# A gated mix of linear attention and a Fourier block on one core: stores, adds and accumulators moved within a hand-written order

## The chip, the core and the metric

The kernel runs on one core of a Trainium2 chip. The metric is the device time of one execution in microseconds (us), as the median of several runs. TensorE (PE in the profile) multiplies matrices out of SBUF into PSUM; VectorE (DVE) and ScalarE (ACT) work element by element; GpSimd (POOL) and SyncE (SP) issue DMA transfers here. Every engine works through its own list of instructions in the order of that list, so an instruction that waits holds up all that stand behind it on the same engine.

## What is computed

The reference, cut to what matters (S = 2048 rows, D = 576 columns, 32 heads of 18):

```python
g = sigmoid((x * gate_w).sum(-1))
q, k, v = split(x @ wqkv)                       # per head
pq, pk = phi(q), phi(k)                         # phi(t) = t+1 if t>0 else exp(t); + 1e-6
o = (pq @ (pk.T @ v)) / (pq @ sum(pk) + 1e-6)   # linear attention
a = o @ wo
b = Cr @ (x @ Wr.T) - Ci @ (x @ Wi.T)           # real part of a 2-d Fourier transform
out = g * a + (1 - g) * b
```

## The kernel before, in words

Every float32 product is made out of three products of split operands: each operand is written as a high part (made by ScalarE, `hi_of`, L179) and a low part (VectorE subtracts, `lo_of`, L189), and high x high, high x low and low x high are added up in PSUM. Four of the products (q, and those with W_r, W_i, Cr and Ci) are also done by a scheme with seven products in place of eight half-size ones: left and right operands are combined by adds on VectorE first (`add`, L199), into seven "forms". A group of rows t and its partner t + 8 make a pair; there are eight pairs.

The stages in order of time:

1. k's product for 16 row groups, and the gate (L574, L209).
2. The product with x of the k-features, 20 steps (five column groups c of x times four groups q of rows; L754). Each step loads a chunk (`xg_load`), makes its high part on ScalarE (`xg_next`) and queues its low part, which VectorE does at the next step's `tick()`. TensorE reads a chunk two steps after its high part was queued. Beside this run, step by step, the preparations for later stages: `turn` says at which step which of four generators goes on by one piece: `a`, `b`, `c` are the three parts of W_q (`right_here`: load, adds, adds, high part, low part in two pieces), `x` is the form of pair 6, `p` the form of the remainders (32 columns of each half, stored to DRAM).
3. q's product in 56 slots (`q_slot`, TensorE at L929), seven products for each of eight pairs, taken in four "quads" of two pairs: (6, 2), (3, 4), (0, 5), (7, 1). Each slot is seven matmuls, under a microsecond. What comes out of PSUM goes through sums on VectorE, an exponential on ScalarE (L938, or L942 and L943) and a last operation on VectorE (L939, L944) into one of 16 accumulators `acc` of [128, 576]. `plan` says behind which slot what else is queued: the forms of pairs 7, 0 and 1 (`left[k]`, five pieces each: two adds, two adds, high part, two low parts; their loads are `begin_left`, L366 on POOL), the stores of forms to DRAM (`here[k].store`, L398 on POOL, seven DMAs for a pair, held until the last exponential queued so far is done), the normalising steps (`norm`), and `m`, the splitting of the output matrix M (five parts; two of them end in an accumulating DMA on POOL, L909, the last one is the remainder's high part on ScalarE and low part on VectorE).
4. The output product, 16 iterations i (L1345 on): the next accumulator is transposed on TensorE (L840), split into qs (ScalarE, VectorE), multiplied with M (L209), scaled into `acc[i]` by ScalarE (L1356) and stored to `att` (L1358, on POOL). `hidden.make_w(k)` makes the seven parts of W_r at given iterations (high part on ScalarE, low part on VectorE), and SyncE loads remainders (`load_rest`, L1111) and forms (`load_pair`, `load_x`, L1117) for the next stage.
5. The product of x with W_r (L1134), that with Cr (L1290), and the same with W_i and Ci.

SBUF is one arena, and every tile's place is an offset given by hand. Dependences follow from overlapping places: whoever writes a place waits for all that still read it. The accumulators lie in a row from ACC_AT, 2,304 bytes each; pair 6's form lies at ACC_AT + 22784, so it overlaps accumulators 9 to 15. The third quad's results are accumulators 8 to 11, the fourth's 12 to 15. W_r's parts have seven places, of which `Layout.w` picks one for each part; place 4 covers SLOT_AT + 43776 to 49536, place 6 SLOT_AT + 32256 to 38016. The remainder of pair 2 is loaded to T_AT + 60416.

The order on ScalarE, VectorE and SyncE is as written in the program; on TensorE it is as written in the q product and from the W_r product on. Elsewhere, and on POOL, a planner sets it.

Of the kernel before, what the change touches and what calls it, by code (L numbers as in the profile page):

```python
# [8 lines left out]
F = mybir.dt.float32  # L9
# [5 lines left out]
P = 128  # L15
S, D, H, DH = 2048, 576, 32, 18
# [51 lines left out]
T_AT = 0  # L68
ACC_AT = T_AT + NP * TPAIR
SLOT_AT, SLOT = ACC_AT + NT * D * 4 + 256, 7 * BS * P * 4  # L70
# [21 lines left out]
class Layout:  # L92
# [32 lines left out]

    def w(self, k):
        if not self.swap:
            k = (k + 4) % 7
        if k < 4:
            return WF_AT + k * WF  # L130
        if self.swap and k == 6:
            return SLOT_AT + 3 * SLOT
        return SLOT_AT + 14 * XF + XR + (6 - k) * WF + (1024 if self.swap else 0)
# [3 lines left out]
def kernel(  # L137
# [24 lines left out]
    def at(offset, shape, dtype=F, name="t"):  # L162
        count[0] += 1
        t = nc.alloc_sbuf_tensor_at(f"{name}_{count[0]}", list(shape), dtype,
                                    offset=base + offset)
        return t.ap()
# [8 lines left out]
    def bank():  # L175
        return psum.tile([P, 512], F, tag="bank", name="bank")
# [17 lines left out]
    def tick():  # L194
        while pending:
            pending.pop(0)()
# [9 lines left out]
    def run(ps, pairs):  # L206
        pairs = list(pairs)
        for n, (a, b) in enumerate(pairs):
            nc.tensor.matmul(ps, a, b, start=(n == 0), stop=(n == len(pairs) - 1))  # L209

    def half(h):
        return slice(h * HALF, (h + 1) * HALF)
# [37 lines left out]
    acc = [at(ACC_AT + i * D * 4, [P, D], F, "acc") for i in range(NT)]  # L250
# [26 lines left out]
    def steps(xs, rhs):  # L277

        for c in range(KC):
            yield xs[:, c], rhs(c)  # L280
            yield xs[:, c], rhs(5 + c)
            yield xs[:, 5 + c], rhs(c)
        yield xs[:, 4], rhs(4)
        yield xs[:, 9], rhs(4)
# [169 lines left out]
    def right_here(src, rest, places, last, temp):  # L454
# [3 lines left out]
        def piece(k):  # L458
# [24 lines left out]
            else:  # L483
                rows = slice(32, 64)
                lo_of(hi[rows], r[rows], hi[rows])

        return w, [piece(k) for k in range(3)]

    def right_raw(src, rest, o, o_rest):
# [21 lines left out]
    def go(gen, n=1):  # L511
        for _ in range(n):
            next(gen, None)
# [7 lines left out]
    done = []  # L521
# [174 lines left out]
    here, forms, rests = {}, {}, {}  # L696

    def begin_left(k, o):
        here[k] = Left(k, o, done[-1])
        if k < NP:  # L700
            forms[k] = here[k].c
# [8 lines left out]
    def load_rest_q(p, o, queue=nc.sync):  # L710
        rests[p] = at(o, [P, 7, P], R, "xr")
        n = min(NP * 96 - p * 96, P)
        queue.dma_start(out=rests[p].bitcast(F)[:n], in_=xrest[p * 96:p * 96 + n])
# [6 lines left out]
    def load_two(*places):  # L720
        for p, o in places:
            forms[p] = at(o, [P, 7, 2, 2 * P], R, "xf")
        for a, b in ((2, 4), (0, 2), (4, 7)):
# [2 lines left out]

    turns = dict(p=rest_forms(), a=wq_pieces[0], b=wq_pieces[1], c=wq_pieces[2], x=left_of(6, False))
    turn = {4: "p", 5: "p", 6: "p", 7: "p", 8: "pap", 9: "pa", 10: "paxc", 11: "pxpaac",
            12: "pcxcb", 13: "xbb", 14: "b", 15: "x", 17: "b"}

    plan = {
        2: [lambda: begin_left(NP, ACC_AT)],
# [100 lines left out]
    def transposed(i):  # L833

        xs, _ = new_xs("qs", qs_ring)
        banks = [bank(), bank()]
        twice = twices.pop(0)
        for c in range(5):
            a = acc[i][:, c * P:(c + 1) * P] if c < KC else twice.rearrange("p a b -> p (a b)")
            nc.tensor.transpose(banks[c // KC][:, (c % KC) * P:(c % KC + 1) * P], a, ident)  # L840
        hi_of(xs[:, 0:4], banks[0])
        lo_of(xs[:, 5:9], banks[0], xs[:, 0:4])
        hi_of(xs[:, 4], banks[1][:, :P])
        lo_of(xs[:, 9], banks[1][:, :P], xs[:, 4])
        return xs
# [68 lines left out]
    def m_row(h, j):  # L914
        return ms["hi"][:, j, half(h)] if j <= KC else ms["lo"][:, j - 5, half(h)]
# [16 lines left out]
    def q_feature(t, h, src, plus):  # L932
        dst = acc[place[t]][:, half(h)]

        def act():
            e = at(es.next(), [P, HALF], F, "e")
            if plus:
                done.append(nc.scalar.activation(e, src, AF.Exp, bias=less))  # L938
                dves.append(lambda: nc.vector.scalar_tensor_tensor(  # L939
                    dst, e, 1.0, src, op0=ALU.min, op1=ALU.max))  # L940
                return
            nc.scalar.activation(e, src, AF.Relu, scale=-1.0)  # L942
            done.append(nc.scalar.activation(e, e, AF.Exp, scale=-1.0))  # L943
            dves.append(lambda: nc.vector.scalar_tensor_tensor(  # L944
                dst, src, 0.0, e, op0=ALU.max, op1=ALU.add))

        feats.append(act)

    def q_slot(n, s, q):
# [35 lines left out]
        elif q == 3:  # L985
            add(sa, x, sa)
            q_feature(p, 1, sa, 1)

    pz_ring.at = [SLOT_AT + 47488]
    for g in (0, 1, 4):  # L990
        load_wo(g)
# [6 lines left out]
    def spread():  # L998
# [17 lines left out]
        16: [lambda: move_m(2), lambda: move_m(0, nc.gpsimd), lambda: move_m(3)],  # L1016
        17: [lambda: move_m(4), lambda: move_m(1, nc.gpsimd)],
        25: [lambda: begin_left(1, T_AT + 35840)],
        26: [lambda: here[6].store(slice(0, 4), done[-1]),
             lambda: here[6].store(slice(4, 7), done[-1])],  # L1020
        30: [spread],
        31: [lambda: load_rest_q(7, T_AT + 80384), lambda: load_rest_q(1, T_AT + 108928)],
        44: [lambda: here[7].store(slice(0, 4), done[-1]),
             lambda: here[7].store(slice(4, 7), done[-1])],
    }
    for k, what in ((7, (10, 11, 13, 15, 20)), (0, (13, 15, 18, 20, 23)),
                    (1, (31, 35, 36, 36, 38)), (None, (25, 27, 30, 41, 43, 45, 48, 48, 49, 52)),
                    ("m", (24, 30, 28, 34, 33))):
        for n, j in enumerate(what):
            f = norm if k is None else m_parts[n] if k == "m" else lambda k=k: go(left[k])  # L1030
            plan.setdefault(j, []).append(f)
# [51 lines left out]
    class Hidden:  # L1083
# [45 lines left out]
        def product(self, ps, p, k, start):  # L1129
            x, (w, wl) = self.x[p, k], self.w[k]  # L1130
            ops = [(x[:, a, c * P:c * P + P], w[:, 2 * c + b]) for c in range(2) for a, b in FULL]
            ops.append((self.rest[p][:96, 6 - k], wl[:96]))
            for n, (a, b) in enumerate(ops):
                nc.tensor.matmul(ps, a, b, start=(start and n == 0), stop=(n == len(ops) - 1),  # L1134
                                 skip_group_check=True)
# [209 lines left out]
    for i, t in enumerate(seq):  # L1345
        qs = nxt
        if i:
            go(norms)
        if i + 1 < NT:
            nxt = transposed(i + 1)  # L1350
        if not i:
            go(norms)
        for h in range(2):
            ps = bank()
            run(ps[:, :HALF], steps(qs, lambda j: m_row(h, j)))
            done.append(nc.scalar.activation(acc[i][:, half(h)], ps[:, :HALF], AF.Copy,  # L1356
                                             scale=gate[:, t:t + 1]))
        nc.gpsimd.dma_start(out=att[t], in_=acc[i])  # L1358
        go(norms)
        tick()  # L1360
        if i == 0 or 2 < i < 7:
            go(wr_make)
        for k, j in ((1, 2), (1, 3), (0, 4), (0, 5)):
            if i == j:
                here[k].store((slice(0, 4), slice(4, 7))[j % 2], done[-1])
        for k, j in enumerate((7, 8, 9, 10, 11, 12, 14)):
            if i == j:
                hidden.make_w(k)
        if i == 4:
            hidden.load_pair(1)  # L1370
        for p, j in ((0, 7), (1, 8), (2, 11), (3, 15)):
            if i == j:
                hidden.load_rest(p)
        if i == 11:
            hidden.load_pair(2)
        if i in (13, 15):
            for k in (0, 2) if i == 13 else (4, 6):
                hidden.load_x(3, k)
# [57 lines left out]
def _layouts(inputs):  # L1436
# [27 lines left out]
    def right(w):  # L1464

        main, rest = halves(w)
        quarters = ((0, 0), (1, 0), (1, 1), (0, 1))
        cols = (slice(0, HALF), slice(HALF, D))
        main = np.stack([main[d][:, :, cols[c]] for d, c in quarters], axis=2)
        rest = np.stack([rest[d][:, cols[c]] for d, c in quarters], axis=1)  # L1470
        return main, np.concatenate([rest] * 3)
# [44 lines left out]
```

## Time and profile before

| what | us |
|---|---|
| median of 3 runs | 721.76 |
| the runs | 721.05 to 722.81 |
| the profiled execution | 724.75 |
| its span, first to last instruction | 723.0 |
| stage 2 (x with the k-features) on TensorE | 65.6 to 132 |
| q's product | 132 to 191 |
| output product | 191 to 258.7 |
| W_r's product | 258.7 to 311.3 |

The profile is of one execution, so durations and times of day ("at 176.5") are of that execution, counted from its first instruction. A row of the timeline reads: start, duration of the group, engine and line, operation, what is written and read, shapes, count, and in brackets how long the engine stood idle before it and what ended that wait. A "landing" is the time from the start of a DMA's issue to its last byte.

### The profile page before, as it was taken

What the parts mean: (1) busy time and instruction counts of PE and PEld (TensorE: products, weight loads), DVE (VectorE), ACT (ScalarE), POOL (GpSimd) and SP (SyncE); (2) the same over time, 40 slices, a digit from 0 to 9 for tenths busy, and PEclk for the clock granted to TensorE, in tenths of its full rate; (3) what the DMA queues carried; (4) which work ended last, traced back from release to release, by engine and by line L of the source; (5) the groups of instructions that cost most, each with busy time, mean ns of one, the idle gap of its engine ahead of it and who ended that gap; (6) DMA issues with size and microseconds to landing.
All of it is one profiled execution on the core that took longest, in us unless ns stands there. A gap on an engine that the chain in (4) does not pass through costs nothing.

```text
span 723.0 us, 13795 instructions
## 1 busy us (share of the span) xinstructions
PE 715.7 (99%) x5390; PEld 714.7 (99%) x5390; DVE 594.8 (82%) x993; ACT 331.1 (46%) x507; POOL 79.0 (11%) x141
## 2 busy tenths in 40 slices
PE   9999999999999999999999999999999999999997
PEld 9999999999999999999999999999999999999997
DVE  5799996477999748899889899757889988788884
ACT  6898355577545535454334233323535333232230
POOL 1122431123252100000010000000000000000000
PEclk9999999999999999999999999999999999999999
DMA  7375799979389557454476666899954543454540
GB/s 257 108 261 190 257 348 323 335 261 250 119 271 411 224 198 276 131 183 144 130 241 209 238 209 208 290 325 400 372 188 136 167 152 123 136 167 154 153 153 34
DMA packets 54093, 157.85 MB, mean 218 GB/s; under 512 B 6884, under 2 KB 9348, under 8 KB 54028
## 3 DMA queue, kind: packets, MB, share of 16 engines
q1 hardware_dynamic: 42524, 117.23, 47.9%
q0 software_dynamic: 11216, 39.32, 15.6%
q8 instruction: 43, 0.70, 0.4%
q10 hardware_dynamic: 288, 0.41, 0.2%
q14 instruction: 22, 0.18, 0.1%
HBM read 117.80 MB, written 36.49 MB: 213 GB/s over the span
## 4 chain that ended last, share of the span: by engine, by line
PE 92%; DMA 3%; DVE 2%; ACT 1%; issue 0%; POOL 0%; DVEq 0%; POOLq 0%
PE bank L1290 49%; PE bank L209 15%; PE bank L1134 15%; PE bank L754 6%; PE bank L929 4%; PE bank L574 2%; PE bank L840 1%; DMA wraw<-in_wq_dram 1%; DMA xm<-xb 1%; DMA xb<-in_xq_dram 1%; ACT xb L179 1%; DVE xb L189 1%; PE bank L235 1%; DVE xb L199 0%; DVE sum L199 0%
## 5 line engine op out<-in xcount | busy, mean ns | idle before, releaser
L1290 PE MATMUL bank<-fh,c 128*128 128x288 f32 x1792 | 355.8, 295 | 0.0
L1290 PEld LDWEIGHTS bank<-fh,c 128*128 128x128 f32 x1792 | 285.9, 188 | 0.1
L1290 PE MATMUL bank<-fl,c 128*128 128x288 f32 x896 | 262.8, 293 | 0.0
L179 ACT ACTIVATE c<-craw 128x1792 fp32r<-128x1792 f32 (+1 forms) x84 | 121.1, 1447 | 171.5 <-DVE craw L199 164.0
L1290 PEld LDWEIGHTS bank<-fl,c 128*128 128x128 f32 x896 | 168.7, 188 | 0.0
L189 DVE TENSOR_TENSOR c<-craw,c 128x1792 fp32r<-128x1792 f32 (+4 forms) x86 | 142.0, 1653 | 1.5 <-ACT c L179 1.4
L199 DVE TENSOR_TENSOR craw<-craw 128x256 f32<-128x256 f32 (+1 forms) x192 | 98.2, 512 | 22.0 <-DMA craw<-in_ci_dram 10.6
L1134 PE MATMUL bank<-wf,xf 128*128 128x288 f32 x630 | 98.5, 296 | 0.0
L1134 PEld LDWEIGHTS bank<-wf,xf 128*128 128x128 f32 x630 | 90.0, 189 | 0.0
L209 PE MATMUL bank<-mw,qs 128*128 128x288 f32 x448 | 63.2, 298 | 0.0
L754 PE MATMUL bank<-pk,c 128*128 128x288 f32 x448 | 61.6, 296 | 1.3 <-DVE c L189 1.3
L754 PEld LDWEIGHTS bank<-pk,c 128*128 128x128 f32 x448 | 60.1, 188 | 1.5 <-DVE c L189 1.5
L209 PEld LDWEIGHTS bank<-mw,qs 128*128 128x128 f32 x448 | 59.9, 188 | 0.1
L209 PE MATMUL bank<-wd,xs 128*128 128x288 f32 (+1 forms) x336 | 44.7, 295 | 0.0
L209 PEld LDWEIGHTS bank<-wd,xs 128*128 128x128 f32 x336 | 44.6, 188 | 0.0
L199 DVE TENSOR_TENSOR ys<-bank,ys 128x288 f32<-128x288 f32 x63 | 28.8, 457 | 17.3 <-PE bank L1290 14.3
L189 DVE TENSOR_TENSOR fl<-fl,fh 128x864 fp32r<-128x864 f32 (+1 forms) x32 | 34.7, 1093 | 6.7 <-ACT fh L179 5.4
L179 ACT ACTIVATE fh<-fl 128x864 fp32r<-128x864 f32 (+1 forms) x32 | 29.8, 949 | 16.4 <-DVE fl L199 16.4
L398 POOL DMA_DIRECT2D xm<-xb x56 | 30.4, 549 | 27.7 <-ACT sum L970 7.9
L1134 PE MATMUL bank<-wf,xr 96*128 96x288 f32 x112 | 33.3, 298 | 0.0
L199 DVE TENSOR_TENSOR ys<-ys,bank 128x288 f32<-128x288 f32 x47 | 21.2, 450 | 13.0 <-PE bank L1290 12.4
L1312 ACT ACTIVATE ys<-bank 128x288 f32<-128x288 f32 x16 | 6.6, 415 | 54.9 <-PE bank L1290 54.9
(133 smaller groups left out, 807.9 us busy)
## 6 DMA issues: line engine op xcount, KB each, us to landing
xf<-xm SPq DMA_DIRECT2D x49, 512.0 KB, 9.0
craw<-in_cr_dram SPq DMA_DIRECT2D x32, 512.0 KB, 3.6
craw<-in_ci_dram SPq DMA_DIRECT2D x32, 512.0 KB, 3.7
xm<-xb POOLq DMA_DIRECT2D x56, 256.0 KB, 4.9
xr<-xr SPq DMA_DIRECT2D x21, 448.0 KB, 8.4
craw<-in_xg_dram SPq DMA_DIRECT2D x20, 256.0 KB, 5.8
att<-acc POOLq DMA_DIRECT2D x16, 288.0 KB, 3.1
row<-att SPq DMA_DIRECT2D x16, 288.0 KB, 4.2
```

Of the source, the lines that this page charges most:

```text
L179: return nc.scalar.activation(dst, src, AF.Copy, bias=bias)
L189: nc.vector.tensor_tensor(out=dst, in0=src, in1=hi, op=ALU.subtract)
L199: nc.vector.tensor_tensor(out=dst, in0=a, in1=b, op=op)
L209: nc.tensor.matmul(ps, a, b, start=(n == 0), stop=(n == len(pairs) - 1))
L235: nc.tensor.matmul(warm[:, :P], ones_f, ones_f, start=True, stop=True)
L398: ins = nc.gpsimd.dma_start(out=xforms[self.k][:, f], in_=self.c.bitcast(F)[:, f])
L574: nc.tensor.matmul(ps[i], x[:, i * P:(i + 1) * P], wkt.row(h, j), start=(c == 0 and n == 0), stop=(c == KC and n == 1))
L754: nc.tensor.matmul(ps[h][:, :HALF], t[:, a, k], pk[s][:, b, half(h)], start=(s == 0 and n == 0), stop=(s == NT - 1 and n == len(passes) - 1))
L840: nc.tensor.transpose(banks[c // KC][:, (c % KC) * P:(c % KC + 1) * P], a, ident)
L929: nc.tensor.matmul(ps, a, b, start=(start and n == 0), stop=(stop and n == len(ops) - 1), skip_group_check=True)
L1134: nc.tensor.matmul(ps, a, b, start=(start and n == 0), stop=(n == len(ops) - 1), skip_group_check=True)
L1290: nc.tensor.matmul(ps[q], c[x][:, l, k], factors[p](y, f), start=(p == 0 and i == 0), stop=(p == NP - 1 and i == 2))
```

## The change

It has five parts:

- `turn`: W_q's part `b` goes on at steps 13 (twice), 14, 15 and 17; before, at 12, 13 (twice), 14 and 17. Its first adds come behind the step-13 low part of x's chunk and behind a piece of pair 6's form.
- Accumulators 9, 10 and 11 get places of their own: SLOT_AT + 47488, T_AT + 62720 and T_AT + 60416.
- The stores of pair 6's form are queued behind slot 36; before, behind slot 26.
- Pair 1's form: second adds behind slot 33 (before 35), high part behind 35 (before 36). The last part of M's split goes behind slot 40 (before 33).
- W_r's parts 0 and 2 exchange places, part 3 is made at iteration 9 and part 2 at iteration 10 (before, the other way round). Part 2's new place overlaps that of accumulator 9.

```diff
     def w(self, k):
         if not self.swap:
-            k = (k + 4) % 7
+            k = (6, 5, 4, 0, 1, 2, 3)[k]
...
     turn = {4: "p", 5: "p", 6: "p", 7: "p", 8: "pap", 9: "pa", 10: "paxc", 11: "pxpaac",
-            12: "pcxcb", 13: "xbb", 14: "b", 15: "x", 17: "b"}
+            12: "pcxc", 13: "xbb", 14: "b", 15: "xb", 17: "b"}
...
+    for i, o in ((9, SLOT_AT + 47488), (10, T_AT + 62720), (11, T_AT + 60416)):
+        acc[i] = at(o, [P, D], F, "acc")
     pz_ring.at = [SLOT_AT + 47488]
...
         25: [lambda: begin_left(1, T_AT + 35840)],
-        26: [lambda: here[6].store(slice(0, 4), done[-1]),
-             lambda: here[6].store(slice(4, 7), done[-1])],
         30: [spread],
         31: [lambda: load_rest_q(7, T_AT + 80384), lambda: load_rest_q(1, T_AT + 108928)],
+        36: [lambda: here[6].store(slice(0, 4), done[-1]),
+             lambda: here[6].store(slice(4, 7), done[-1])],
...
-                    (1, (31, 35, 36, 36, 38)), (None, (25, 27, 30, 41, 43, 45, 48, 48, 49, 52)),
-                    ("m", (24, 30, 28, 34, 33))):
+                    (1, (31, 33, 35, 36, 38)), (None, (25, 27, 30, 41, 43, 45, 48, 48, 49, 52)),
+                    ("m", (24, 30, 28, 34, 40))):
...
-        for k, j in enumerate((7, 8, 9, 10, 11, 12, 14)):
+        for k, j in enumerate((7, 8, 10, 9, 11, 12, 14)):
             if i == j:
                 hidden.make_w(k)
```

## The prediction

> **What bounds the kernel now.** I read the page first, then the waits of TensorE, then the rows in order of time around each wait.
>
> ```profile
> PE 715.7 (99%) x5390; PEld 714.7 (99%) x5390; DVE 594.8 (82%) x993; ACT 331.1 (46%) x507; POOL 79.0 (11%) x141
> ...
> PE bank L754 <- DVE c L189: 1.3, 1, 1.3
> ...
> PE bank L929 <- DVE xb L189: 1.2, 1, 1.2
> ```
>
> TensorE works 99% of the span, and no matmul goes or shortens in this change. Behind the start only these two waits stand to be won, so the case is two places of about 1.5 us each, and what is late next at each.
>
> **First place, W_q's adds (steps 12 to 15).** TensorE, then VectorE:
>
> ```profile
> 113.73 0.76 PE L754 MATMUL bank<-pk,c 128*128 128x288 f32 x4
> 115.81 8.29 PE L754 MATMUL bank<-pk,c 128*128 128x288 f32 x60 [1.31 <-DVE c L189]
> ...
> 109.86 2.25 DVE L189 TENSOR_TENSOR wb<-wraw,wb 32x2016 fp32r<-32x2016 f32 x1 [1.41 <-ACT wb L179]
> 114.19 0.95 DVE L199 TENSOR_TENSOR wraw<-wraw 128x288 f32<-128x288 f32 x2 [2.09 <-DMA wraw<-in_wq_dram]
> 115.06 0.69 DVE L189 TENSOR_TENSOR c<-craw,c 128x512 fp32r<-128x512 f32 x1
> 115.67 1.22 DVE L189 TENSOR_TENSOR xb<-xb,xb 128x1024 fp32r<-128x1024 f32 x1
> ```
>
> Step 14 starts at 113.73, issues four matmuls and stops for the low part of its own chunk (115.06). VectorE was free from 112.11 but stood 2.09 before W_q's first two adds, whose load had not landed; the low part was queued behind them. The price: a matmul's row lasts 0.30 and the pace is (8.29 - 0.30) / 59 = 0.135, so the fourth started at 113.73 + 0.76 - 0.30 = 114.19, the fifth was due at 114.33 and came at 115.81: 1.48. The first interval behind a wait is about 0.1 longer than the pace (below: four matmuls in 0.80, (0.80 - 0.30) / 3 = 0.17), so the place costs 1.58.
>
> After the change the two adds stand behind that low part and behind the sixth pair's low part. The chunk's low part runs from 112.1 to 112.8, 1.5 ahead of its reader; the pair's to 114.0; then the same load is awaited, the two pairs of adds now run back to back to 114.19 + 0.95 + 0.87 = 116.0, and the next chunk's low part ends at 116.6 or 116.7. Its reader is the fifth matmul of step 15: 20 matmuls are left of step 14, so 114.33 + 24 x 0.135 = 117.6. Cover 0.9. W_q's high part then starts at 116.0 in place of 117.78 though it stands a step later, so its readers get it no later. **1.58 goes**; what is late next is the same load, were it 0.9 later.
>
> **Second place, pair 1's form (slots 31 to 41).** TensorE, VectorE, ScalarE:
>
> ```profile
> 174.91 0.43 PE L929 MATMUL bank<-wb,xb 128*128 128x288 f32 x2
> 176.50 0.80 PE L929 MATMUL bank<-wb,xb 128*128 128x288 f32 x4 [1.16 <-DVE xb L189]
> ...
> 170.38 0.76 DVE L199 TENSOR_TENSOR xb<-xb 128x256 f32<-128x256 f32 x2 [2.19 <-DMA xb<-in_xq_dram]
> 171.18 0.76 DVE L189 TENSOR_TENSOR mw<-mraw,mw 64x576 fp32r<-64x576 f32 x1
> ...
> 172.34 0.88 DVE L199 TENSOR_TENSOR xb<-xb 128x256 f32<-128x256 f32 x2
> ...
> 175.22 1.23 DVE L189 TENSOR_TENSOR xb<-xb,xb 128x1024 fp32r<-128x1024 f32 x1 [1.27 <-ACT xb L179]
> ...
> 170.84 0.40 ACT L972 ACTIVATE sum<-bank 128x288 f32<-128x288 f32 x1
> ...
> 173.25 1.94 ACT L179 ACTIVATE xb<-xb 128x1024 fp32r<-128x1024 f32 x2 [0.25 <-DVE xb L199]
> ```
>
> Slot 41 was due for its third matmul at 174.91 + 0.13 + 0.13 = 175.17 and got it at 176.50: 1.33, with the restart 1.43. The chain behind it: the load of pair 1 lands (170.38), two adds, M's last low part and a sum between, two adds, high part on ScalarE, low part to 176.45.
>
> I keep this profile's clock and take the first gain off both sides (the work here is released by TensorE's own products). With the load landing as now, the second adds follow the first: 170.38 to 171.15 to 171.95. ScalarE is free from 171.24, so the high part runs 171.98 to 173.93 and the low part ends at 175.2, 1.25 earlier than now. TensorE at 175.17 loses 0.05 and a restart: the place alone gives 1.43 - 0.17 = **1.26**.
>
> But that isn't what arrives at the end. The stretch behind it:
>
> ```profile
> 176.00:196.00 20.00, 19.74 (x45) 1.00 0.43 131
> ...
> 191.32 3.95 PE L209 MATMUL bank<-mw,qs 128*128 128x288 f32 x28
> 195.57 4.11 PE L209 MATMUL bank<-mw,qs 128*128 128x288 f32 x28
> ...
> 195.48 0.89 DVE L189 TENSOR_TENSOR qs<-bank,qs 128x512 fp32r<-128x512 f32 x2
> ```
>
> From 176 to 196 VectorE is busy 19.74 of 20 us (the first row, VectorE alone), and iteration 1 of the output product needs the low part made at 195.48: it lasts 4.11, not 3.95. So VectorE has no slack there, and TensorE gains only what VectorE gains. VectorE leaves pair 1's low part 1.25 earlier, but M's last low part moves from the idle stretch (slot 33) into the packed one (slot 40): 0.76, some 0.68 start to start, as neighbours overlap by 0.08. Lead 1.25 - 0.68 = 0.57; I take **0.55**, for the moved high part on ScalarE is just in time. Bounds: 0, were the load 0.6 later because M's accumulating moves now run beside its tail, and 1.4 (the first rival). M's own cover is long: iteration 0 starts at 191.32.
>
> **The stores of pair 6** (slot 26 to 36; seven issues on POOL):
>
> ```profile
> 163.47 1.45 POOL L366 DMA_DIRECT2D xb<-in_xq_dram  x2 [10.85 <-ACT sum L968]
> 164.91 1.67 POOL L398 DMA_DIRECT2D xm<-xb  x3
> ...
> 172.53 0.89 POOL L909 DMA_DIRECT2D mw<-minus  x1 [0.85 <-issue]
> ...
> 182.61 3.80 POOL L398 DMA_DIRECT2D xm<-xb  x7 [7.91 <-ACT sum L970]
> ...
> 189.54 0.45 DVE L939 SCALAR_TENSOR_TENSOR acc<-e,sum 128x288 f32<-128x288 f32 x1
> ```
>
> They now wait for slot 36's exponential (about 174.4) and issue in 3.8, as pair 7's do, or in 6.8, as theirs do now: done by 178 to 181. Behind them on POOL stand pair 7's stores, held till 182.6 anyway. M's two accumulating moves come out ahead of them, some 4 us earlier. The accumulators that still lie in pair 6's place are first written about 189.5; the three others have places of their own, and this costs no instruction. All of this at nothing.
>
> Does the load of pair 1 land earlier without these stores behind it? Its landings here, in pair 6's case and in pair 7's, then of the first store, and what stood around the other two:
>
> ```profile
> DMA to landing us min/median/max: 4.6/5.3/6.1
> ...
> DMA to landing us min/median/max: 4.1/4.5/5.0
> ...
> DMA to landing us min/median/max: 7.1/7.4/7.8
> ...
> DMA to landing us min/median/max: 6.8/6.8/6.8
> ...
> 92.51 0.59 POOL L398 DMA_DIRECT2D xm<-xb  x1
> ...
> 130.65 4.67 SPq L725 DMA_DIRECT2D xf<-xm  x6
> ```
>
> Pair 6's load had stores right behind it (92.51) and landed in at most 5.0; pair 7's had none but six loads of SyncE beside it (130.65) and took 7.8. The first store behind pair 1 landed at 164.91 + 6.8 = 171.7, after the load at 170.3. So what slows the load is SyncE's transfers, which stay: I take no gain, with 0.9 as the other end. The Trainium skill, DMA: Bandwidth & Descriptors, section Queues, rings and completion order, says that one queue's descriptors are consumed in ring order on each DMA engine and that an engine takes turns between queues; by it the stores, issued later on the same queue, can't pass the load. The landings above agree; by it the sum is 2.13, without it up to 2.98.
>
> **W_r's order and places.** Part 2 is now made at iteration 10 in a place that overlaps accumulator 9, and the remainder of pair 2 is loaded over accumulators 10 and 11.
>
> ```profile
> 234.67 0.54 POOL L1358 DMA_DIRECT2D att<-acc  x1 [3.72 <-ACT acc L1356]
> ...
> 238.56 1.00 ACT L179 ACTIVATE wf<-wraw 128x576 fp32r<-128x576 f32 x2
> ...
> 240.08 0.89 DVE L189 TENSOR_TENSOR qs<-bank,qs 128x512 fp32r<-128x512 f32 x2
> ...
> 242.53 3.96 PE L209 MATMUL bank<-mw,qs 128*128 128x288 f32 x28
> ...
> DMA to landing us min/median/max: 2.4/3.1/7.8
> ...
> 220.56 9.60 SPq L1117 DMA_DIRECT2D xf<-xm  x6
> ...
> 258.72 52.59 PE bank L1134 x392
> ```
>
> The new wait on ScalarE: att of accumulator 9 leaves at 234.67; the part is made at 238.56. It must land within 3.9; att takes 2.4 to 7.8 (row of L1358). Queued behind on ScalarE is qs for iteration 12, read by its fifth matmul at 242.53 + 0.53 = 243.06, made by 240.08 + 0.69 = 240.77: ScalarE may be held 2.3, so a landing up to 6.2 is free. The new wait on SyncE: that remainder waits for att of accumulator 11, and behind it stand the loads of pairs 2 and 3 (the six at 220.56 and more), so they start near 243. Pair 2 is read at 258.72 + 2 x 52.59 / 8 = 271.9: cover 28. And since they no longer run at 220 to 243, att at 234.67 should land nearer 2.4. I cost both at nothing; at the row's 7.8 the first would be 1.6.
>
> **Sum.** 1.58 + 0.55 = 2.13. The profiled execution takes 724.75 (span 723.0, 1.75 around it), the median of the runs shown is 721.76; the difference goes off each: 722.6 with the profiler, **719.6** without.
>
> **Rivals.**
> - *The stores did slow the load.* At 0.9 earlier (169.5) the second adds end at 171.1, ScalarE starts at 171.24, the low part ends at 174.35: VectorE's lead is 2.1 - 0.68 = 1.4, and TensorE takes 1.4. Total 2.98: 718.8. Against it: the landings above.
> - *The first wait comes back a step later.* The adds, now four in a row, stand before the next chunk's low part; if W_q's load lands 0.9 later than here, TensorE waits at step 15, and each further 1 us costs 1. At 2 us later: 720.7. Against it: nothing ahead of that load changes.
> - *The waits are the profiler's.* The profiled execution is 2.99 longer than the median, and both waits are 3.01. If plain runs hardly have them, nothing is won: 721.8. For it: that coincidence. Against it: the runs themselves differ by 1.76, which one such wait would explain.
>
> The last one needs a row first, the form loads of SyncE between 220 and 235:
>
> ```profile
> DMA to landing us min/median/max: 11.1/11.3/13.7
> ```
>
> - *Slower: ScalarE held by att of accumulator 9.* Above 6.2 each us costs TensorE one, and 2.13 is eaten at 8.3. If att took those loads' longest, 13.7, 7.5 would be lost: 727.1. Against it: those loads now come later.
>
> **How the numbers follow.** Forecast 0.47 (719.6, its own 719.0 to 720.2), load earlier 0.24, first wait back 0.11, waits of the profiler 0.13, slower 0.05. The range 718.5 to 721.3 leaves out the slower case, most of the profiler's and a tail of the earlier load. A measurement of this kernel can tell about 0.3% (2.17 us, that is 719.59) from no change: half of the forecast and all of the earlier load lie beyond, 0.49; slower 0.05; the same 0.46.
>
> **What would show it.** Right: no wait of TensorE at L754; at L929 none or under 0.2; the output product's iteration 1 above 4.11, by about 0.7; pair 1's load landing in about 6; pair 6's stores after M's accumulating moves; SyncE's loads of pairs 2 and 3 from about 243. Wrong: a wait at step 15, a wait of ScalarE before wf at iteration 10, a load under 5.2, or iteration 1 still at 4.11.

## The result and the profile after

| | us |
|---|---|
| kernel after, median of 22 runs | 721.58 (720.87 to 722.80) |
| kernel before, 22 runs beside them | 722.85 (721.05 to 724.90) |
| ratio, 95% interval | 0.9985 (0.9978 to 0.9992) |
| profiled execution of after, its span | 721.35, 719.6 |

The change makes the kernel 0.15% faster, 1.1 to 1.3 us: less than the 2.13 of the prediction, and the time lies 0.28 above the top of its range. Against the profiled execution of before the profile shows 3.40 less. That gap is the subject of what follows.

The page of the kernel after, then the waits of its TensorE (behind the start, neither of the two waits is left):

```profile
PE 714.8 (99%) x5390; PEld 714.2 (99%) x5390; DVE 595.1 (83%) x993; ACT 330.9 (46%) x507; POOL 79.0 (11%) x141
```

```profile
engine line waited for: us in total, times, longest us
PE bank L235 <- POOL ones_f L231: 1.2, 1, 1.2
```

First place, VectorE in order of time. The two low parts come first, and W_q's four adds follow without a wait:

```profile
109.54 2.25 DVE L189 TENSOR_TENSOR wb<-wraw,wb 32x2016 fp32r<-32x2016 f32 x1 [1.41 <-ACT wb L179]
111.82 0.69 DVE L189 TENSOR_TENSOR c<-craw,c 128x512 fp32r<-128x512 f32 x1
112.43 1.22 DVE L189 TENSOR_TENSOR xb<-xb,xb 128x1024 fp32r<-128x1024 f32 x1
113.56 1.80 DVE L199 TENSOR_TENSOR wraw<-wraw 128x288 f32<-128x288 f32 x4
```

Second place, VectorE, then POOL, then the landings of pair 1's load. VectorE stands 1.01 for that load (2.19 before), and M's last part is now at 175.12. Behind the load, POOL has M's two moves and only then the stores:

```profile
167.39 1.56 DVE L199 TENSOR_TENSOR xb<-xb 128x256 f32<-128x256 f32 x4 [1.01 <-DMA xb<-in_xq_dram]
...
171.14 1.23 DVE L189 TENSOR_TENSOR xb<-xb,xb 128x1024 fp32r<-128x1024 f32 x1 [1.01 <-ACT xb L179]
...
175.12 0.76 DVE L189 TENSOR_TENSOR mw<-mraw,mw 64x576 fp32r<-64x576 f32 x1
```

```profile
161.50 1.45 POOL L366 DMA_DIRECT2D xb<-in_xq_dram  x2 [10.85 <-ACT sum L968]
166.84 0.93 POOL L909 DMA_DIRECT2D mw<-minus  x1 [3.88 <-ACT sum L970]
169.41 0.86 POOL L909 DMA_DIRECT2D mw<-minus  x1 [1.65 <-ACT sum L972]
171.89 2.73 POOL L398 DMA_DIRECT2D xm<-xb  x5 [1.62 <-ACT e L938]
```

```profile
DMA to landing us min/median/max: 4.3/4.7/5.1
```

The load landed 5.1 us after its issue at the latest, not in about 6, and so below the 5.2 that the prediction named as a sign of being wrong. TensorE in iterations 0 and 1 of the output product, and SyncE:

```profile
187.93 3.95 PE L209 MATMUL bank<-mw,qs 128*128 128x288 f32 x28
...
192.32 4.17 PE L209 MATMUL bank<-mw,qs 128*128 128x288 f32 x28
```

```profile
213.42 29.43 SPq L1113 DMA_DIRECT2D xr<-xr  x3
242.95 4.08 SPq L1119 DMA_DIRECT2D xf<-xm  x6
```

Iteration 1 takes 4.17; it was forecast about 0.7 above the 4.11 of before. The loads of the next stage start at 242.95, as forecast.

ScalarE has one new wait, not at iteration 10 but at the last part of W_r, made at iteration 14:

```profile
255.41 1.02 ACT L179 ACTIVATE wf<-wraw 128x576 fp32r<-128x576 f32 x2 [3.04 <-DMA att<-acc]
```

### The profile page after: what moved, and what is told of

It reads as the page before. It is cut to its first block, busy times and chain, and to the rows that moved or that the text cites. A ratio compares the mean times of both kernels' runs of the same rounds, so it can differ in the third digit from the quotient of the medians.

```text
span 719.6 us, 13794 instructions
## 1 busy us (share of the span) xinstructions
PE 714.8 (99%) x5390; PEld 714.2 (99%) x5390; DVE 595.1 (83%) x993; ACT 330.9 (46%) x507; POOL 79.0 (11%) x141
## 4 chain that ended last, share of the span: by engine, by line
PE 99%; DVE 0%; DVEq 0%; issue 0%; POOL 0%; POOLq 0%
PE bank L1292 49%; PE bank L209 15%; PE bank L1136 15%; PE bank L754 8%; PE bank L929 7%; PE bank L574 2%; PE bank L840 1%; PE bank L235 1%; PE bank L690 0%; DVE row L1308 0%; DVE ys L199 0%; PE bank L693 0%; DVEq L1514 0%; POOL ones_f L231 0%; POOL ident masks.py:197 0%
```

## The experiments

Three theories stood against each other. *Fixed prices*: the two waits are a constant part of the time (1.58 and 1.43), and the stores of pair 6 don't touch pair 1's load. *Landings*: each wait is what is left when a load lands, which differs from one execution to the next, so a median run loses less than the profiled one. *Stores*: the stores right behind pair 1's load delay it, so that their move, not the form's, empties the second wait.

The expectations of the first four runs call the landings the chance theory, and "my theory" there is that the stores don't touch the load. In the expectations from before_2 on, theory A is the landings together with the stores, B the fixed prices, and D that the accumulators' places do it.

All times, each beside runs of the kernel before on the same chip (a single run for before_2 and after_2). The ratio and its interval are as recorded; the ratio differs from the quotient of the two medians by up to 0.07%:

| kernel | median (range) | before | ratio, interval |
|---|---|---|---|
| e_adds | 721.52 (720.75 to 722.90) | 722.42 | 0.9985 (0.9974 to 0.9997) |
| e_form | 723.14 (721.81 to 723.99) | 722.42 | 1.0006 (0.9997 to 1.0015) |
| e_stores | 721.64 (720.82 to 723.23) | 722.42 | 0.9989 (0.9979 to 1.0000) |
| e_st26 | 721.62 (721.00 to 722.73) | 722.42 | 0.9991 (0.9983 to 1.0000) |
| before_2 | 721.64 | 722.30 | |
| after_2 | 722.48 | 722.30 | |
| e_two | 721.16 (720.60 to 721.95) | 722.30 | 0.9984 (0.9975 to 0.9993) |
| e_m33 | 721.08 (720.45 to 722.05) | 722.30 | 0.9988 (0.9978 to 0.9998) |
| e_places | 722.05 (720.85 to 724.35) | 722.52 | 0.9997 (0.9986 to 1.0008) |
| e_noadds | 722.62 (721.11 to 724.03) | 722.52 | 1.0000 (0.9989 to 1.0011) |
| after_3 | 721.45 (720.65 to 722.07) | 722.52 | 0.9986 (0.9977 to 0.9996) |
| e_two_2 | 720.98 (720.56 to 721.43) | 722.52 | 0.9972 (0.9961 to 0.9983) |

An interval is 1.2 to 1.7 us wide, so I read the places from the traces. All these kernels run the same 5,390 matmuls. So the start of TensorE's 700th, 1000th, 2000th and last matmul (at 95.4, 134.2, 265.4 and 714.9 in e_two_2), less that of the same one in e_two_2, tells where an execution lost time: in the start, at the first place, at the second with the output product's first steps, or later. "Landing" is the longest of pair 1's load, "issue" when POOL issued W_q's load.

```
kernel     adds  stores form M   start  first  second rest   landing  issue
before     old   26     old  33  0.81   1.65   1.58   0.15   6.1      106.06
before_2   old   26     old  33  0.08   1.05   0.01  -0.07   4.6      103.90
e_places   old   26     old  33  0.79   1.23   1.87  -0.09   6.4      105.83
e_adds     new   26     old  33  0.93   0.00   0.95  -0.09   5.5      104.65
e_form     old   26     new  40  0.21   1.55   1.46   0.03   5.9      104.68
e_st26     new   26     new  40  0.01   0.00   1.15  -0.09   5.9      103.71
e_stores   old   36     old  33  0.09   0.43   0.23  -0.01   4.6      104.32
e_two      new   36     old  33  1.20   0.00   0.00   0.03   4.1      104.16
e_two_2    new   36     old  33  0      0      0      0      4.1      103.77
e_m33      new   36     new  33  0.58   0.00   0.00   0.65   4.4      104.64
after      new   36     new  40  0.49   0.00   0.37  -0.09   5.1      104.65
after_2    new   36     new  40  0.80   0.35   0.37   0.40   4.5      106.40
after_3    new   36     new  40  0.22   0.00   0.36  -0.09   4.5      104.50
e_noadds   old   36     new  40  0.37   1.68   0.37   0.51   4.4      105.54
```

**e_adds**: the kernel before with W_q's adds a step later, nothing else.

```diff
-            12: "pcxcb", 13: "xbb", 14: "b", 15: "x", 17: "b"}
+            12: "pcxc", 13: "xbb", 14: "b", 15: "xb", 17: "b"}
```

> The kernel before with W_q's adds a step later and nothing else. Fixed-price theory (each wait of TensorE costs in every execution what the profiled one showed): 1.6 us faster than before, so all of the 1.27 that the whole change gave and more. Chance theory (the waits come from DMA landings that differ from execution to execution, and the profiled execution of before, 724.75, was near the slowest of 22): 0.3 to 0.8 us faster in the median, and the slowest executions go. In the trace no wait at L754 by either; the wait at L929 of about 1 us stays.

It gives 0.9 us. Its waits of TensorE (the line of the start left out), and VectorE's first adds of pair 1:

```profile
PE bank L929 <- DVE xb L189: 0.5, 1, 0.5
```

```profile
168.24 0.76 DVE L199 TENSOR_TENSOR xb<-xb 128x256 f32<-128x256 f32 x2 [1.38 <-DMA xb<-in_xq_dram]
```

The first wait is gone. The 0.9 lies next to the 0.3 to 0.8 of the chance theory, but the interval (0.2 to 1.9) holds the fixed 1.6 as well. The second wait, untouched by this edit and expected to stay at about 1, is 0.5 where the profile of before has 1.2; the load landed in 5.5 against 6.1.

**e_form**: the kernel before with the form of pair 1 earlier and M's last part behind slot 40; the stores stay.

```diff
-                    (1, (31, 35, 36, 36, 38)),
+                    (1, (31, 33, 35, 36, 38)),
...
-                    ("m", (24, 30, 28, 34, 33))):
+                    ("m", (24, 30, 28, 34, 40))):
```

> The kernel before with pair 1's second adds and high part earlier and M's last part behind slot 40; pair 6's stores stay behind slot 26. Fixed-price theory with VectorE as the limit behind it: 0.55 us faster, no wait over 0.2 at L929, the output product's iteration 1 about 0.7 longer than 4.11 less what the first wait leaves. Chance theory: 0.3 to 0.6 faster. Stores theory (the stores behind pair 1's load on POOL slow it): the load still lands about 6 us after its issue, and the gain is at most 0.3.

No gain: 0.7 above the kernel before, though the interval holds no change. The waits of TensorE, and VectorE:

```profile
PE bank L754 <- DVE c L189: 1.2, 1, 1.2
...
PE bank L209 <- ACT qs L179: 0.4, 1, 0.4
```

```profile
169.45 1.56 DVE L199 TENSOR_TENSOR xb<-xb 128x256 f32<-128x256 f32 x4 [1.82 <-DMA xb<-in_xq_dram]
```

The wait at L929 is gone, but 1.46 is lost all the same, most of it in iteration 1 of the output product. VectorE stood 1.82 for the load, and what it was late with then comes due some 25 us later at another line.

**e_stores**: the kernel before with the accumulators' places, the stores behind slot 36 and W_r's order; adds, form and M as before.

```diff
-        26: [lambda: here[6].store(slice(0, 4), done[-1]),
-             lambda: here[6].store(slice(4, 7), done[-1])],
...
+        36: [lambda: here[6].store(slice(0, 4), done[-1]),
+             lambda: here[6].store(slice(4, 7), done[-1])],
```

> The kernel before with the three accumulators' places, pair 6's stores behind slot 36 and W_r's new order, but the old order of pair 1's form, M and W_q. My theory: the stores don't slow pair 1's load, so it lands about 6 us after its issue as before and the time is the same within 0.3 us. Stores theory: the load lands about 5 us after its issue, the wait at L929 shrinks by about 1 us, and the kernel is 0.5 to 1 us faster.

0.8 less, at the edge of its interval. VectorE at the two places:

```profile
112.26 0.95 DVE L199 TENSOR_TENSOR wraw<-wraw 128x288 f32<-128x288 f32 x2 [0.87 <-DMA wraw<-in_wq_dram]
```

```profile
166.96 0.76 DVE L199 TENSOR_TENSOR xb<-xb 128x256 f32<-128x256 f32 x2
```

With the old form and the old place of M, VectorE doesn't wait for pair 1 at all, and the second place costs 0.23. The first place is as before, and yet it costs 0.43 in this execution: the stand for W_q's load is 0.87, not 2.09.

**e_st26**: the kernel after with the stores back behind slot 26.

```diff
-        36: [lambda: here[6].store(slice(0, 4), done[-1]),
-             lambda: here[6].store(slice(4, 7), done[-1])],
+        26: [lambda: here[6].store(slice(0, 4), done[-1]),
+             lambda: here[6].store(slice(4, 7), done[-1])],
```

> The changed kernel with pair 6's stores put back behind slot 26. My theory: the same time as the changed kernel within 0.3 us (so some 1.3 faster than before), pair 1's load landing about as in the changed kernel. Stores theory: pair 1's load lands 1 us later than in the changed kernel, and the time is 0.5 to 0.9 us longer than the changed kernel's.

By its time hardly to be told from the kernel after (0.8 under before, where that is 1.1 to 1.3 under). The landings of pair 1's load, VectorE, and TensorE:

```profile
DMA to landing us min/median/max: 4.5/5.2/5.9
```

```profile
167.78 1.56 DVE L199 TENSOR_TENSOR xb<-xb 128x256 f32<-128x256 f32 x4 [1.77 <-DMA xb<-in_xq_dram]
```

```profile
192.53 4.17 PE L209 MATMUL bank<-mw,qs 128*128 128x288 f32 x28 [0.46 <-ACT qs L179]
```

The late load is back, and with it a wait in the output product. What GpSimd's DMA queue moved from the first issue of pair 1's load to its landing, first in e_st26, then in e_stores (packets, MB, share of the 16 DMA engines' time):

```profile
q0 software_dynamic: 266, 0.90, 46.2%
```

```profile
q0 software_dynamic: 160, 0.52, 33.7%
```

The load itself is two transfers of 256 KB, 0.52 MB, and in e_stores the queue carried nothing else. With the stores behind it the queue had moved 0.38 MB more before the load landed.

**before_2**, the kernel before once more:

> The kernel before once more, for one more profiled execution. Theory A (the waits hang on when a load lands, and that differs from execution to execution; pair 6's stores right behind pair 1's load delay it): W_q's first sum starts 7.9 to 8.8 us after its load is issued and TensorE waits 0 to 1.3 us at L754; pair 1's first sum starts 6.3 to 6.9 us after its load is issued and TensorE waits 0.5 to 1.2 us at L929; the time lies anywhere from 721.0 to 725. Theory B (the prediction: fixed prices): 1.3 and 1.2 us again at these two lines, and 724.7 us.

Its waits of TensorE, VectorE at both places, and pair 1's landings:

```profile
PE bank L754 <- DVE c L189: 0.7, 1, 0.7
```

```profile
112.88 0.95 DVE L199 TENSOR_TENSOR wraw<-wraw 128x288 f32<-128x288 f32 x2 [1.50 <-DMA wraw<-in_wq_dram]
```

```profile
167.47 0.76 DVE L199 TENSOR_TENSOR xb<-xb 128x256 f32<-128x256 f32 x2 [0.26 <-DMA xb<-in_xq_dram]
```

```profile
DMA to landing us min/median/max: 4.5/4.5/4.6
```

The same kernel, 3.11 us shorter than its first profiled execution: 0.73 in the start, 0.60 at the first place, 1.57 at the second, 0.22 later. Here the second wait doesn't exist, though the stores stand right behind the load and theory A had expected 0.5 to 1.2 for it. Two more expected bounds fell: the first sum of W_q came 8.98 after the issue (8.8 expected), that of pair 1 5.32 (6.3 expected).

**after_2**, the kernel after once more:

> The kernel after once more. Theory A: no wait at L754 and none at L929; pair 1's first sum starts 5.4 to 6.0 us after its load is issued, about 0.9 us less than with the stores right behind the load; 0.2 to 0.4 us lost in the second step of the output product; 721.0 to 722.4 us, the rest of the spread from the start of the kernel. Theory B: the same two waits gone, pair 1's sums 6.9 us after the issue, as with the stores behind it, and 0.7 us lost in the output product.

VectorE at the first place:

```profile
115.29 1.81 DVE L199 TENSOR_TENSOR wraw<-wraw 128x288 f32<-128x288 f32 x4 [1.31 <-DMA wraw<-in_wq_dram]
```

W_q's load was issued at 106.40, 1.75 later than in the first profile of after; the adds stand for it, and 0.35 is lost, no longer at step 14 but at step 15. In the prediction this is a rival; it is real, and shows in one of the eight executions with the new adds. Theory A had expected no loss here, and the time, 722.48, is just above its 722.4. As much is lost in the output product as in the other executions of this kernel (0.37).

**e_two**: the kernel after with the old form and M's part behind slot 33, that is W_q's adds and the stores' move without the rest of the q product's edits.

```diff
-                    (1, (31, 33, 35, 36, 38)),
+                    (1, (31, 35, 36, 36, 38)),
...
-                    ("m", (24, 30, 28, 34, 40))):
+                    ("m", (24, 30, 28, 34, 33))):
```

> The kernel after without the earlier form of pair 1 and with M's last part at slot 33: W_q's sums a step later, the stores ten products later, the places and the order of W_r. Theory A: the stores' move alone empties the second wait, so that the form's move is worth nothing: no wait at L754 and none above 0.2 us at L929, pair 1's sums 5.4 to 6.0 us after the issue, no loss in the output product, and the time of the kernel after or up to 0.3 us less (721.3 to 721.6). Theory B: the wait of 1.16 us at L929 stands, 722.1 to 722.8.

No wait of TensorE is left at L929 and nothing is lost in the output product. The stores' move empties the second place without the form's edits (that the places don't do it is shown by e_places, below); by fixed prices the wait of 1.16 would have stood. The time, 721.16, is 0.14 under the range that was expected.

**e_m33**: the kernel after with M's last part back behind slot 33.

```diff
-                    ("m", (24, 30, 28, 34, 40))):
+                    ("m", (24, 30, 28, 34, 33))):
```

> The kernel after with M's last low part back at slot 33. Theory A: the 0.2 to 0.4 us of the output product go, nothing else changes, 721.2 to 721.6. Theory B: VectorE's 0.68 us at that place goes, 720.9.

The time, 721.08, lies between the two expectations (721.2 to 721.6 and 720.9), so the trace has to tell them apart. The 0.37 of the output product goes; iteration 1 of e_m33 is as long as iteration 0 (4.17 in the kernel after):

```profile
192.28 3.95 PE L209 MATMUL bank<-mw,qs 128*128 128x288 f32 x28
```

This execution loses 0.65 later, at the product with Cr, which no edit here touches; after_2 and e_noadds lose 0.40 and 0.51 behind the 2000th matmul, most of it there too.

**e_places**: the kernel before with the accumulators' places and W_r's order, stores at slot 26.

```diff
+    for i, o in ((9, SLOT_AT + 47488), (10, T_AT + 62720), (11, T_AT + 60416)):
+        acc[i] = at(o, [P, D], F, "acc")
...
-            k = (k + 4) % 7
+            k = (6, 5, 4, 0, 1, 2, 3)[k]
...
-        for k, j in enumerate((7, 8, 9, 10, 11, 12, 14)):
+        for k, j in enumerate((7, 8, 10, 9, 11, 12, 14)):
```

> The kernel before with the three accumulators' places and the order of W_r's parts alone; pair 6's stores stay at slot 26. Theory A (the stores right behind pair 1's load slow it): the load's longest landing is 5.5 to 6.1 us, as in four of the five executions so far with these stores behind it, TensorE waits up to 1.2 us at L929, and the time is that of the kernel before within 0.4 us. Theory D (the places are what helps): longest landing 4.1 to 5.1 us, no wait at L929, and 0.8 us less than the kernel before.

The places and the order are worth nothing that can be told (0.9997). Waits of TensorE and pair 1's landings:

```profile
PE bank L929 <- DVE xb L189: 1.4, 1, 1.4
...
PE bank L754 <- DVE c L189: 0.9, 1, 0.9
```

```profile
DMA to landing us min/median/max: 4.9/5.7/6.4
```

With the stores right behind it the load is the latest of all (6.4, above the expected 5.5 to 6.1). So what helped in e_stores is the stores' place.

**e_noadds**: the kernel after with W_q's adds at their old steps.

```diff
-            12: "pcxc", 13: "xbb", 14: "b", 15: "xb", 17: "b"}
+            12: "pcxcb", 13: "xbb", 14: "b", 15: "x", 17: "b"}
```

> The kernel after with W_q's adds at their old steps. Theory A: W_q's first sum waits for its load and TensorE for it, 0 to 1.3 us at L754 by the execution, 1.0 us on average, so the median is 0.7 to 1.2 us above that of the kernel after; pair 1's load lands within 5.1 us and L929 shows no wait. The prediction's fixed price: 1.58 us above the kernel after. If the first place were worth nothing: the time of the kernel after.

1.17 above the kernel after on the same chip (722.62 against 721.45), within the 0.7 to 1.2 of the landings and under the fixed 1.58. With runs from 721.11 to 724.03 the median alone doesn't rule the 1.58 out; the traces do, by what the old adds cost from one execution to the next (0.43 to 1.68). Its waits of TensorE, and pair 1's landings:

```profile
PE bank L754 <- DVE c L189: 1.3, 1, 1.3
```

```profile
DMA to landing us min/median/max: 3.8/4.1/4.4
```

**after_3** and **e_two_2**, the kernels after and e_two side by side:

> The kernel after once more, beside the others on one chip: 1.0 to 1.3 us less than the kernel before by the medians; no wait at L754 or L929 over 0.3 us; the second step of the output product loses 0.2 to 0.4 us against the kernel without the form's move.

> The kernel after without the earlier form of pair 1 and with M's last part at slot 33, once more beside the kernel after. Theory A: 0.2 to 0.4 us less than the kernel after by the medians, pair 1's longest landing under 5.2 us, no wait at L929 and none in the output product. The prediction, by which the form's move brings 0.55 us: 0.55 us more than the kernel after.

e_two_2 is faster than the kernel before (0.9972). Against the kernel after it is 0.47 us less by the medians, where 0.2 to 0.4 was expected and the traces differ by 0.36 at the second place; the two ranges overlap and no interval for this pair is on record. So by the traces the move of M's last part is what the kernel after could do without.

## Why the prediction was wrong

**The sum was taken off the wrong base; this step failed.** It said of the 2.13 that "the difference goes off each": off the profiled execution and off the median. But both terms were read from one execution that held both waits nearly at their largest. The working itself was good for that execution: at the first place it lost 1.65 by the table, priced 1.58; at the second 1.58, of which the wait was priced 1.43. A median run doesn't hold that much. Over the six executions with the old adds the first place costs 1.26 on average (0.43 to 1.68), over the eight with the new ones 0.04; by the times the difference is 0.90 (e_adds) and 1.17 (e_noadds). Over the four with stores and form as before the second place costs 1.10 (0.01 to 1.87). The runs of before hinted at it: the profiled execution lay 2.99 above their median. Their lowest run, 721.05, may be one in which the waits hardly happened, though no trace of it is there. A forecast of 719.6 lay 1.45 below it; no run of any kernel here went under 720.33. The prediction saw that coincidence and gave it to a rival ("the waits are the profiler's"), whose 721.8 is near the result, by luck: it takes nothing off a base that was itself too low. That rival's reason is not what happened: the waits are in plain runs as well, or e_noadds wouldn't be 1.17 behind.

**And the base itself was low.** 721.76 was the median of three runs; later groups have 722.30 to 722.85. Beside the 22 runs, the forecast missed by 1.95: 1.09 from the base (722.85 - 721.76) and 0.86 from the sum (2.13 - 1.27).

**First place.** Right in its mechanism and its lines; the cover of 0.9 held in seven of eight executions. The size is 1.2 by the traces, 0.9 and 1.17 by the times of e_adds and e_noadds, where 1.58 stood.

**The stores "at nothing".** Wrong. The prediction found that "what slows the load is SyncE's transfers". Pair 1's longest landing is 5.73 on average in the six executions with the stores right behind it (4.6 to 6.4) and 4.46 in the eight without (4.1 to 5.1): 1.27 less. With the old form that takes the second place from 1.10 to 0.08. The comparison with pair 6's load, which has stores behind it and lands early, misled; one store stood right behind it, three stand here, but why that load escaped is not shown. The other reason was that the first store landed (171.7) after the load (170.3). That is the order of whole transfers. What GpSimd's queue moved from the issue of pair 1's load to its landing, in the kernel before and in before_2, tells more:

```profile
q0 software_dynamic: 304, 1.02, 47.4%
```

```profile
q0 software_dynamic: 161, 0.53, 41.5%
```

In the profile of before 0.50 MB of the stores' data had moved before the load of 0.52 MB was complete. So it is in all five executions with a late load (5.5 to 6.4; the queue moved 0.71 to 1.03 MB). In before_2, the one with the stores behind the load in which it landed early (4.6), next to nothing of them had moved, and the second wait is missing; what held them back there isn't shown. In the eight without the stores nothing had (0.52). Packet by packet, the queue had moved as much as the load's size 0.8 to 1.4 us before the landing in the five, and 0.4 to 0.6 in the other nine. It isn't that the DMA engines were fuller: from 163 to 166 us, with the load under way in both, they were 0.86 busy in e_st26 and 0.96 in e_stores.

The Trainium skill, DMA: Bandwidth & Descriptors, section Queues, rings and completion order, was read as if order in the ring protected the load. The same section says that data descriptors carry no barrier, so that a later one may finish its write before an earlier one. The 1.27 and the 1.02 MB show that being first in the queue doesn't keep a load's landing free of what is queued behind. Whether the stores pass the load on one DMA engine, or some engines run ahead of others, is not shown.

**The form.** Together with M's move it was to bring 0.55. With the stores where they were, it takes the wait from L929, but the second place still costs 1.31 (1.46 and 1.15) against 1.10. So the doubt beside "the place alone gives 1.26" was right: what VectorE is late with comes due later, as argued from its 19.74 of 20 us. No run moves the form alone with the stores at their old place. **M's last part**, priced 0.68, costs 0.37 (0.36 or 0.37 in the three executions of the kernel after and in e_noadds, e_m33 0.00). So the net of the second place by the traces is 1.10 - 0.37 = 0.73, near the 0.55 forecast by luck, for it comes another way: the stores gain 1.02 and the form's edits give 0.29 back. The times are too coarse to confirm that net: e_noadds, which has it without the first place, measured no change (0.9989 to 1.0011).

**W_r, att and SyncE at nothing.** Right for TensorE: e_places shows no change, and no execution of the kernel after loses more than 0.02 between iteration 2 of the output product and the 3300th matmul. Accumulator 9's att landed 2.3 us after its issue (5.8 in the kernel before), as expected. What the prediction didn't see: the loads that now start at 242.95 run beside later att stores, that of accumulator 13 took 6.8 (issued at 248.53; 2.4 before), and ScalarE stands 3.04 for it at 255.41. So the rival "ScalarE held by att" came at another iteration, where it cost TensorE nothing.

**What stays open.** By the traces the whole is 1.22 + 0.73 = 1.95, by the medians 1.27 and 1.07. That difference has no shown cause; few executions were traced, and the start alone, which no edit here touches, varies by 1.2. (One small sum of the prediction is off: half of 0.47 and 0.24 make 0.475, where 0.49 stands.)

## What to carry to other kernels

A wait in a profile is the wait of one execution: where the profiled execution lies above the median by about as much as the waits add up to, trace the kernel a second time before pricing them, and distrust a forecast that lies far below the lowest run. Where a load's reader is late, look at what is queued right behind the load as well as ahead of it. And a stall taken from one place can come due at another line when the engine behind it is busy 99% of the next 20 us, as VectorE was here, so an edit belongs in the stretch where that engine idles.

## What the runs showed of the hardware

- Executions differ by up to 1.2 us before the 700th matmul, where no edit changes anything (e_two and e_two_2, one kernel on two chips; 0.9 between e_adds and e_st26 on one chip), and by the landing of single loads: W_q's landed in 6.6 to 8.2, pair 1's in 4.1 to 5.1 at the longest even without stores behind it.
- The load of W_q is issued when the stores ahead of it have landed, so its issue moves as well, from 103.71 to 106.40; TensorE's wait follows from both.
- Stores queued right behind a load on GpSimd's DMA queue can have moved up to 0.5 MB of their data before the load is complete, and the load then landed in 5.5 to 6.4 us instead of 4.1 to 5.1.
